# Slots in token order, three early gathers and six late tiles in a fused attention and two-MLP kernel

## The chip, the core and the metric

One core of a Trainium2 chip runs the whole program. The metric is the time of one execution in device microseconds (us). A kernel's time is the median of its timed runs; beside them stands one profiled execution, from which all durations of parts are read. The engines are TensorE (PE; PEld is its weight load), VectorE (DVE), ScalarE (ACT), GpSimd (POOL) and SyncE (SP, here an issuer of DMAs).

## The reference, cut to what matters

Three parts follow each other. Attention between x (8 batches of 512 tokens) and a state of 32 rows per batch gives 8 x 544 = 4352 rows of 512 numbers: 512 x rows and then 32 state rows for each batch. A softplus MLP (512 to 2048 to 512) runs over all of them. Then each row is given to one of eight experts and goes through that expert's MLP:

```python
logits = x @ w_gate
order = np.argsort(-logits.flatten())
for idx in order:
    tok, e = (int(idx) // E, int(idx) % E)
    if assigned[tok] >= 0 or counts[e] >= cap:
        continue
    assigned[tok] = e
    counts[e] += 1
...
for e in range(E):
    mask = assigned == e
    h = np.maximum(x[mask] @ w1[e], 0.0)
    out[mask] = h @ w2[e]
```

With cap = 544, each expert gets exactly 544 rows. The order of the rows inside one expert is free: they are gathered, worked on, and written back to their places.

## The kernel before

**Main loop.** The first MLP runs over 128 slots s = 16 b + ft (8 batches, 16 tiles of 128 hidden columns each), and over 16 state tiles that hold the 256 state rows of all batches. A slot computes h (mlp1), softplus g in steps on ACT and DVE, splits g in a high and a low part (g_hi on ACT or DVE, g_lo at L557 on POOL or DVE), and adds three matmuls of 512 columns to each of four outputs (mlp2: hi x hi, lo x hi, hi x lo).

**Tail.** The second matmuls of the last LATE = 4 slots (12 each) and of the state tiles are held back: mlp2_rest() issues them one at a time. State tiles come as two passes of 16 (j = 0, 1 for the two halves of the state rows, 3 matmuls a tile, L582, L584, L586). When pass j is finished, y_state(j) copies the result to SBUF (L637, DVE) and writes it to y_d in DRAM in four pieces (L640, SP for j = 0, SP and ACT for j = 1). split(i + 1) computes g_hi and g_lo of the next tile when tile i starts.

**Routing.** route(ph) finds the next expert and its 544 rows by a search over seven digits of a threshold, a chain of short DVE steps (v, mk, df, ...) and small matmuls (L1044 counts, L1061 sums). Then finish() turns the mask of the chosen rows into slots: M2 holds the rows surely chosen and, beside them, the ties at the threshold; matmuls with a triangular matrix give each row its rank; four DVE operations make the slot sl, two shifts split it, and ohl, a17 and R follow. R's 17 matmuls (L928) sum up to ixs and idx, the list of row numbers (one yield, "slots", lies between R and these matmuls). The route of the first expert runs between the held-back matmuls: step i is followed by BETWEEN[i] of them; at "slots" all that are left are issued (rest(99)), before R's matmuls.

**Gathers and experts.** gather(0) issues indirect DMAs on POOL: xg piece a gets the rows of y_d named by column a of idx (five pieces: 4 x 128 and 32). Each piece is turned by four transposes (L1186), ACT makes yTh (L1189) and DVE yTl (L1190). yTh and yTl lie in memory that the finished first MLP used. The expert's weights w1 are loaded by load_w1 (one DMA of 2 MB, L1115) and split in eight pieces, w1h on ACT (L1158) and w1l on POOL or DVE (L1159). An expert then has 16 units of 12 matmuls (L1277), (ft, half); unit u of the first expert needs piece u for u below 7. The second matmul of the expert (L1322) follows.

**What sets the order.** Strings written by hand: BEGIN is worked off before the first unit, AFTER[u] behind unit u. In the kernel before, x is gather of pieces 0 and 1, y the gather of 2 to 4 and the load of w2, s a w1 piece with w1l on POOL, v one with w1l on DVE, t a group of transposes, r the next step of route(1). Each engine executes its instructions in the order in which they stand; a wait holds up all that stands behind it on that engine.

## Time and profile before

| | us |
|---|---|
| Median of 3 runs | 1209.81 |
| Lowest and highest | 1209.26, 1211.1 |
| The profiled execution | 1206.22 |
| Its span (first to last instruction) | 1204.4 |
| TensorE busy | 1148.3 (95%) |
| DVE, ACT, POOL busy | 649.8, 640.6, 484.4 |
| Mean granted clock of TensorE | 0.99 |

The span leaves 1.82 us of the profiled execution outside. All places in time below are us from the span's start. The tail begins at about 701, the first expert's units at 755.8. In rows in order of time, a start and a duration are followed by engine, line, operation, output <- inputs and, where the engine sat idle before, by how long and what released it. Matmul durations overlap: two that follow each other start 0.23 us apart (512 columns at full clock), though each lasts 0.39.

### The profile page before, as it was taken

To read this page: it belongs to the slowest core of one execution; us is meant where nothing else is said; L and a number is where in the kernel's file an instruction comes from. 1 tells how busy PE (TensorE), PEld (TensorE's weight loads), DVE (VectorE), ACT (ScalarE), POOL (GpSimd) and SP (SyncE) were. 2 spreads that over 40 slices of the span, in tenths; PEclk is the share of its full clock that TensorE was granted. 3 is DMA by queue.
4 is the path that set the end of the run, shared out by engine and by line. 5 is a ranking of instruction groups with operands and counts; after the bars stand their busy time and mean duration, and the time that the engine had idled before them with its cause. 6 is when DMAs were issued, how large, how long until landed. Compare 5 with 4: busy or idle time off the path is not lost.

```text
span 1204.4 us, 21169 instructions
## 1 busy us (share of the span) xinstructions
PE 1148.3 (95%) x8256; PEld 905.3 (75%) x8256; DVE 649.8 (54%) x1744; ACT 640.6 (53%) x1277; POOL 484.4 (40%) x472
## 2 busy tenths in 40 slices
PE   4798999999999999999999997999999999999996
PEld 1566677777677777777777765979797988889895
DVE  6998435463363533634434266776685767641120
ACT  3776666666676666766766732533333333343330
POOL 0333423232232232322344435645646555556531
PEclk9998999999999999999999999899999999999999
DMA  7454021111201201012000003250523425234201
GB/s 245 141 193 142 1 71 36 54 53 36 70 1 42 64 29 55 23 36 70 1 18 19 1 18 123 91 197 25 200 82 143 136 80 180 106 119 133 92 18 38
DMA packets 51060, 95.77 MB, mean 80 GB/s; under 512 B 4624, under 2 KB 19088, under 8 KB 50960
## 3 DMA queue, kind: packets, MB, share of 16 engines
q1 hardware_dynamic: 45232, 76.46, 19.4%
q0 software_dynamic: 5632, 17.83, 4.4%
q8 instruction: 65, 1.06, 0.4%
q14 instruction: 35, 0.29, 0.1%
q10 hardware_dynamic: 96, 0.13, 0.0%
HBM read 76.58 MB, written 17.83 MB: 78 GB/s over the span
## 4 chain that ended last, share of the span: by engine, by line
PE 79%; DVE 10%; issue 6%; POOL 2%; ACT 1%; DMA 1%; SPq 0%; POOLq 0%; DVEq 0%; ACTq 0%
PE p_h L491 13%; PE p_y L1322 12%; PE p_y L575 8%; PE p_y L577 8%; PE p_y L579 8%; PE p_y L1277 7%; PE p_h L1277 6%; PE p_bg L460 2%; PE p_y L582 2%; PE p_bg L502 2%; PE p_y L586 2%; PE p_y L584 2%; PE p_h L1186 1%; DVE c_a L198 1%; PE p_bg L1044 1%
## 5 line engine op out<-in xcount | busy, mean ns | idle before, releaser
L557 POOL TENSOR_TENSOR g_lo<-g,g_hi 128x512 fp32r<-128x512 f32 x127 | 164.1, 1293 | 324.6 <-ACT g_hi L554 268.1
L575 PE MATMUL p_y<-g_hi,wo_hi 128*128 128x512 f32 x448 | 185.6, 414 | 0.0
L577 PE MATMUL p_y<-g_hi,wo_lo 128*128 128x512 f32 x448 | 178.3, 398 | 3.6 <-POOL wo_lo L237 3.6
L579 PE MATMUL p_y<-g_lo,wo_hi 128*128 128x512 f32 x448 | 176.4, 394 | 0.0
L554 ACT ACTIVATE g_hi<-g 128x512 fp32r<-128x512 f32 x126 | 79.6, 632 | 118.5 <-DVE g L546 84.7
L546 DVE SCALAR_TENSOR_TENSOR g<-p_h,t_sp 128x512 f32<-128x512 f32 x128 | 87.5, 684 | 98.1 <-ACT t_sp L534 97.6
L575 PEld LDWEIGHTS p_y<-g_hi,wo_hi 128*128 128x128 f32 x448 | 85.1, 190 | 49.1 <-ACT t_sp L526 12.6
L1322 PE MATMUL p_y<-w2h,h2h 128*128 128x512 f32 x256 | 105.0, 410 | 0.0
L491 PE MATMUL p_h<-at_hi,P_hi 128*128 128x512 f32 x256 | 103.6, 405 | 1.4 <-DVE g L546 1.4
L491 PE MATMUL p_h<-at_hi,P_lo 128*128 128x512 f32 x256 | 101.6, 397 | 0.0
L491 PE MATMUL p_h<-at_lo,P_hi 128*128 128x512 f32 x256 | 101.5, 397 | 0.0
L1322 PE MATMUL p_y<-w2l,h2h 128*128 128x512 f32 x256 | 101.4, 396 | 0.0
L1322 PE MATMUL p_y<-w2h,h2l 128*128 128x512 f32 x256 | 101.2, 395 | 0.0
L577 PEld LDWEIGHTS p_y<-g_hi,wo_lo 128*128 128x128 f32 x448 | 85.3, 191 | 20.7 <-POOL wo_lo L237 4.9
L579 PEld LDWEIGHTS p_y<-g_lo,wo_hi 128*128 128x128 f32 x448 | 85.3, 190 | 19.4
L1330 POOL DMA_INDIRECT out_dram<-ot,idx x40 | 38.7, 969 | 143.8 <-ACT ot L1328 72.5
L526 ACT ACTIVATE t_sp<-p_h 128x512 f32<-128x512 f32 x128 | 75.4, 589 | 27.8 <-PE p_h L491 27.0
L1159 POOL TENSOR_TENSOR w2l<-s2w,w2h 128x512 fp32r<-128x512 f32 x64 | 81.6, 1291 | 13.1 <-ACT w2h L1158 12.3
L534 ACT ACTIVATE t_sp<-t_sp 128x512 f32<-128x512 f32 x128 | 80.9, 632 | 4.1
L1159 POOL TENSOR_TENSOR w1l<-s1w,w1h 128x512 fp32r<-128x512 f32 x63 | 80.1, 1297 | 6.0 <-ACT w1h L1158 5.2
L533 ACT ACTIVATE t_sp<-t_sp 128x512 f32<-128x512 f32 x128 | 80.7, 631 | 2.3
L1277 PE MATMUL p_y<-yTl,w1h 128*128 128x288 f32 (+1 forms) x256 | 77.3, 302 | 0.0
(282 smaller groups left out, 2611.0 us busy)
## 6 DMA issues: line engine op xcount, KB each, us to landing
s1w<-in_moe_w_dram SPq DMA_DIRECT2D x8, 2048.0 KB, 8.3
s2w<-in_moe_w_dram SPq DMA_DIRECT2D x8, 2048.0 KB, 9.1
st<-in_moe_w_in_dram SPq DMA_DIRECT2D x16, 512.0 KB, 4.1
xT<-in_x_t_dram SPq DMA_DIRECT2D x16, 512.0 KB, 4.4
st<-in_moe_w_out_dram SPq DMA_DIRECT2D x16, 512.0 KB, 3.8
xt<-in_x_s_dram SPq DMA_DIRECT2D x8, 1024.0 KB, 5.5
y_d<-yz SPq DMA_DIRECT2D x48, 128.0 KB, 3.5
y_d<-s_g SPq DMA_DIRECT2D x8, 128.0 KB, 2.5
```

What stands on the lines that cost most here:

```text
L491: PE.matmul(h, l[:, f0:f0 + 128], r[:, par, :], start=(n == 0), stop=(n == 5))
L533: A.activation(t, t, AF.Exp, scale=-1.0)
L534: A.activation(t, t, AF.Ln, bias=1.0)
L546: V.scalar_tensor_tensor(g[:, :w], hps.pop(s)[:, :w], 0.0, tsp.pop(s)[:, :w], op0=OP.max, op1=OP.add)
L554: A.activation(hi[:, c], g[:, c], AF.Copy)
L557: (G if on[1] == "G" else V).tensor_tensor(lo[:, c], g[:, c], hi[:, c].bitcast(F32), op=OP.subtract)
L575: PE.matmul(yb[j], wo_hi[:, ft, c], hi, start=st, stop=False)
L577: PE.matmul(yb[j], wo_lo[:, ft, c], hi, start=False, stop=False)
L579: PE.matmul(yb[j], wo_hi[:, ft, c], lo, start=False, stop=sp)
L1159: eng.tensor_tensor(lo, src, hi.bitcast(F32), op=OP.subtract)
L1277: PE.matmul(p[:, :w], l[:, k, f], r[:, k, c], start=(n == 0), stop=(n == 11))
L1322: PE.matmul(p, l[:, ft, c], r[:, ft, :], start=(n == 0), stop=(n == 23))
```

## The change

Slots are given out in the order of rows, ties included. M2 gets one more column between the two halves, tri2 replaces the corner of the triangular matrix that ranked all ties behind all sure rows, and finish() computes the slot with a constant SKIP, in six short DVE operations where there were four (room, val, sl2, sl3, sl, U). So the first expert's first three pieces hold rows from the front of y_d.

Three gathers of the first expert are therefore issued earlier: at "slots" ROWS = 20 held-back matmuls are issued instead of all, 30 are left over for behind R's matmuls, gather(0, range(3)) follows idx at once, then four steps of route(1) with four matmuls each (ROUND), then the rest of the matmuls and y_state(1). The rows of y_d that y_state(1) will write (state rows of batches 4 to 7) are filled with zeros once, in the main loop, by four DMAs on SP.

LATE is 6; the two further g tiles lie in the pool of the state tiles, with their own places in LATE_ON. BEGIN becomes "sttrr", AFTER and W2_FROM change; x is now one gather (pieces 3 and 4), w the load of w2.

```diff
-    LATE = 4
+    LATE = 6
...
-        if s < NX:
+        if 0 <= s - (NX - LATE) < 2:
+            g = stash["pool"].tile([128, 512], F32, name="g2", bufs=2)
+        elif s < NX:
             g = wk.tile([128, 512], F32, name="g", bufs=5)
...
-    LATE_ON = ("VG", "AG", "VG", "AV")
+    LATE_ON = ("VG", "AG", "VG", "AG", "AG", "AV")
...
+            for i in range(4, 8):
+                r0 = i * TB + S
+                SP.dma_start(y_d[r0:r0 + NS], first[3].rearrange("p a b -> p (a b)").bitcast(F32)[0:NS, 0:DM])
...
-        V.scalar_tensor_tensor(val, p[:, 0:2 * NJ], float(CAP), M2, op0=OP.is_lt, op1=OP.mult)
-        sl2 = rt.tile([128, 2 * NJ], F32, name="sl2")
-        V.scalar_tensor_tensor(sl2, p[:, 0:2 * NJ], 1.0, val, op0=OP.add, op1=OP.mult)
-        V.tensor_tensor(U, U, val[:, NJ:], op=OP.subtract)
-        V.scalar_tensor_tensor(sl, sl2[:, 0:NJ], -1.0, sl2[:, NJ:], op0=OP.add, op1=OP.add)
+        room = rt.tile([128, 1], F32, name="room")
+        V.tensor_scalar(room, p[:, NJ:NJ + 1], -1.0, float(CAP), op0=OP.mult, op1=OP.add)
+        val = rt.tile([128, NJ], F32, name="val")
+        V.scalar_tensor_tensor(val, p[:, NJ + 1:2 * NJ + 1], room, M2[:, NJ + 1:], op0=OP.is_lt, op1=OP.mult)
+        sl2 = rt.tile([128, NJ], F32, name="sl2")
+        V.scalar_tensor_tensor(sl2, M2[:, 0:NJ], -float(SKIP), p[:, 0:NJ], op0=OP.mult, op1=OP.add)
+        V.scalar_tensor_tensor(sl3, p[:, NJ + 1:2 * NJ + 1], room, sl2, op0=OP.min, op1=OP.add)
+        V.scalar_tensor_tensor(sl, val, -float(SKIP), sl3, op0=OP.mult, op1=OP.add)
+        V.tensor_tensor(U, U, val, op=OP.subtract)
...
+    ROWS, ROUND = 20, (4, 4, 4, 4)
...
-        rest(99 if at_ == "slots" else BETWEEN[i])
+        rest(ROWS if at_ == "slots" else BETWEEN[i])
         if 0 in RES and 0 not in W1S:
             load_w1(0)
+
+    gather(0, range(3))
+    rgen = routing()
+    for n in ROUND:
+        next(rgen)
+        rest(n)
...
-    BEGIN = "xrrrrrrsyrrttrst"
-    AFTER = ("ssvsrr", "r", "r", "s", "t", "", "t", "s")
-    W2_FROM = 5
+    BEGIN = "sttrr"
+    AFTER = ("rvxsrrw", "rxrs", "rtr", "s", "ts", "rs", "t", "s")
+    W2_FROM = 7
```

Lines after the edits are shifted: L557 becomes L567, L640 L650, L928 L944, L1044 L1064, L1061 L1081, L1133 L1153, L1159 L1186, L1186 L1213, L1190 L1217, L1277 L1303, and L582 to L586 become L592 to L596.

POOL, from the last tiles of the held-back work on: xg<-y_d are the gathers. Before:

```order
L557 TENSOR_TENSOR g_lo<-g,g_hi 128x512
L557 TENSOR_TENSOR g_lo<-s_g,g_hi 128x128 x32
L1133 DMA xg<-y_d,idx 128x512 x2
L1159 TENSOR_TENSOR w1l<-s1w,w1h 128x4x128
L1133 DMA xg<-y_d,idx 128x512 x2
L1133 DMA xg<-y_d,idx 32x512
L1122 MEMSET s2w 1x1
L1159 TENSOR_TENSOR w1l<-s1w,w1h 128x4x128 x5
```

After:

```order
L567 TENSOR_TENSOR g_lo<-g,g_hi 128x512 x3
L567 TENSOR_TENSOR g_lo<-s_g,g_hi 128x128 x27
L1153 DMA xg<-y_d,idx 128x512 x3
L567 TENSOR_TENSOR g_lo<-s_g,g_hi 128x128 x5
L1186 TENSOR_TENSOR w1l<-s1w,w1h 128x4x128
L1153 DMA xg<-y_d,idx 128x512
L1186 TENSOR_TENSOR w1l<-s1w,w1h 128x4x128
L1142 MEMSET s2w 1x1
L1153 DMA xg<-y_d,idx 32x512
L1186 TENSOR_TENSOR w1l<-s1w,w1h 128x4x128 x5
```

The first three gathers now stand ahead of the g_lo of the last five state tiles, and the other two singly between the weight pieces.

TensorE, at the start of the first expert: L1186 and L1213 are transposes of gathered rows, L1061 and L1081 the sum that ends a digit of route(1), L1277 and L1303 the units. Before:

```order
L1186 MATMUL p_h<-ident,xg 128x128 x8
L1061 LDWEIGHTS taken_79
L1061 MATMUL p_bg_7529<-sat_6909,taken_79 128x8
L1186 MATMUL p_h<-ident,xg 128x128 x4
L1277 MATMUL p_y_7553<-yTh,w1h 128x256
L1277 MATMUL p_y_7553<-yTl,w1h 128x256
L1277 MATMUL p_y_7553<-yTh,w1l 128x256
```

After (p_y_7526 is the first unit, p_h the second):

```order
L1303 MATMUL p_y_7526<-yTl,w1h 128x256
L1303 MATMUL p_y_7526<-yTh,w1l 128x256
L1081 LDWEIGHTS taken_79
L1081 MATMUL p_bg_7554<-sat_6886,taken_79 128x8
L1303 MATMUL p_h<-yTh,w1h 128x256
L1303 MATMUL p_h<-yTl,w1h 128x256
L1303 MATMUL p_h<-yTh,w1l 128x256
```

The sum of route(1)'s first digit has moved from ahead of the last transposes to behind the first unit.

DVE, at the first weight piece that it splits itself (w1l), with the answer of that digit (df to mk) ahead of it. Before:

```order
L1190 TENSOR_TENSOR yTl<-p_h,yTh 128x4x128 x2
L1063 TENSOR_REDUCE df<-p_bg_7529 128x1
L1019 TENSOR_SCALAR p_bg_6890<-df 128x1
L74 TENSOR_SCALAR tmp<-p_bg_6890 128x1
L75 SCALAR_TENSOR_TENSOR p_bg_6890<-tmp,p_bg_6890 128x1
L1023 TENSOR_TENSOR p_bg_6890<-pat,p_bg_6890 128x31
L1031 TENSOR_TENSOR mk_6905<-v,p_bg_6890 128x34x31
L1190 TENSOR_TENSOR yTl<-p_h,yTh 128x4x128
L1159 TENSOR_TENSOR w1l<-s1w,w1h 128x4x128
```

After:

```order
L647 COPY yt<-p_y_7337 128x512
L1217 TENSOR_TENSOR yTl<-p_h,yTh 128x4x128 x2
L1069 SCALAR_TENSOR_TENSOR pe<-p_bg_7527,rem_6874 31x8
L1071 SCALAR_TENSOR_TENSOR pe<-p_bg_7527,pe 31x8 x2
L1072 TENSOR_TENSOR sat_6886<-p_bg_7527,pe 31x8
L1083 TENSOR_REDUCE df<-p_bg_7554 128x1
L1039 TENSOR_SCALAR p_bg_6867<-df 128x1
L75 TENSOR_SCALAR tmp<-p_bg_6867 128x1
L76 SCALAR_TENSOR_TENSOR p_bg_6867<-tmp,p_bg_6867 128x1
L1043 TENSOR_TENSOR p_bg_6867<-pat,p_bg_6867 128x31
L1051 TENSOR_TENSOR mk_6882<-v,p_bg_6867 128x34x31
L1186 TENSOR_TENSOR w1l<-s1w,w1h 128x4x128
L1309 SCALAR_TENSOR_TENSOR h2l<-p_y_7526,h2h 128x256
```

Piece 1's w1l stands directly behind the digit's mk; before, DVE's first w1l came behind the third yTl and was piece 5.

## Rows read from the trace of the kernel before

**Rows 1.** Busy us of each engine (x instructions), TensorE's clock, DMA share and GB/s, by stretch.

```profile
640.00:701.00 61.00, 59.34 (x368) 45.88 (x367) 21.01 (x44) 42.31 (x89) 21.82 (x17) 1.00 0.01 2
701.00:743.60 42.60, 40.80 (x238) 28.85 (x239) 31.88 (x126) 11.48 (x35) 21.47 (x45) 1.00 0.21 75
743.60:755.80 12.20, 3.98 (x39) 3.12 (x39) 7.75 (x24) 2.34 (x4) 7.14 (x8) 0.73 0.42 127
755.80:790.00 34.20, 34.15 (x337) 31.93 (x336) 25.19 (x100) 15.63 (x37) 17.78 (x16) 0.95 0.20 66
```

**Rows 2.** TensorE in order of time: start, us, line, out<-in, [idle before <- releaser].

```profile
742.94 0.40 PE L584 MATMUL p_y<-wo_lo,g_hi 128*128 128x512 f32 x1
743.17 0.39 PE L586 MATMUL p_y<-wo_hi,g_lo 128*128 128x512 f32 x1
743.49 0.73 PE L928 MATMUL p_bg<-R,ohl 128*64 128x68 bf16 x17
749.18 0.41 PE L1044 MATMUL p_bg<-ohu,mk 128*128 128x32 bf16 x9 [4.95 <-DVE mk L1031]
751.28 1.12 PE L1186 MATMUL p_h<-ident,xg 128*128 128x128 f32 x4 [1.70 <-DMA xg<-y_d,idx]
...
755.10 1.08 PE L1186 MATMUL p_h<-ident,xg 128*128 128x128 f32 x4 [1.28 <-DMA xg<-y_d,idx]
755.83 0.56 PE L1277 MATMUL p_y<-yTh,w1h 128*128 128x256 f32 x1
...
758.54 0.47 PE L1044 MATMUL p_bg<-ohu,mk 128*128 128x32 bf16 x9
...
760.66 0.18 PE L1061 MATMUL p_bg<-sat,taken 128*128 128x8 bf16 x1
```

**Rows 3.** DVE in order of time, same columns.

```profile
741.51 1.42 DVE L959 TENSOR_TENSOR R<-a,p_bg 128x578 bf16<-128x578 f32 x2
743.60 0.69 DVE L637 COPY yt<-p_y 128x512 f32<-128x512 f32 x1 [0.67 <-PE p_y L586]
...
755.09 0.15 DVE L1063 TENSOR_REDUCE df<-p_bg 128x1 f32<-128x8 f32 x1
...
756.10 1.26 DVE L1031 TENSOR_TENSOR mk<-v,p_bg 128x1054 bf16<-128x1054 f32 x1
...
758.40 0.84 DVE L1159 TENSOR_TENSOR w1l<-s1w,w1h 128x512 fp32r<-128x512 f32 x1 [0.46 <-ACT w1h L1158]
```

**Rows 4.** POOL in order of time, same columns.

```profile
742.43 0.46 POOL L557 TENSOR_TENSOR g_lo<-s_g,g_hi 128x128 fp32r<-128x128 f32 x1 [0.23 <-ACT g_hi L554]
747.56 1.40 POOL L1133 DMA_INDIRECT xg<-y_d,idx  x1 [4.67 <-DVE cu L1004]
749.27 0.95 POOL L1133 DMA_INDIRECT xg<-y_d,idx  x1 [0.31 <-issue]
...
757.41 4.24 POOL L1159 TENSOR_TENSOR w1l<-s1w,w1h 128x512 fp32r<-128x512 f32 x3 [0.99 <-ACT w1h L1158]
```

**Rows 5.** The state rows' writes (L640): SP in order of time; the line's landing.

```profile
731.53 1.74 SPq L640 DMA_DIRECT2D y_d<-yt  x4
...
DMA to landing us min/median/max: 1.6/1.7/2.0
```

**Rows 6.** The second expert's idx on DVE, and its first gather on POOL.

```profile
798.17 0.67 DVE L971 SCALAR_TENSOR_TENSOR idx<-ixs 32x5 int32<-32x5 f32 x4
...
799.63 1.01 POOL L1133 DMA_INDIRECT xg<-y_d,idx  x1 [3.26 <-issue]
```

**Rows 7.** Two stretches at half clock, columns as in Rows 1.

```profile
97.40:100.75 3.35, 3.35 (x12) 2.68 (x9) 3.26 (x7) 2.05 (x4) 1.29 (x1) 0.50 0.48 159
...
749.50:759.50 10.00, 6.73 (x41) 5.91 (x38) 5.66 (x16) 4.66 (x9) 8.22 (x9) 0.50 0.68 199
```

**Rows 8.** ACT in order of time, columns as in Rows 2.

```profile
753.85 0.60 ACT L1189 ACTIVATE yTh<-p_h 128x512 fp32r<-128x512 f32 x1 [0.77 <-PE p_bg L1061]
754.34 0.62 ACT L1158 ACTIVATE w1h<-s1w 128x512 fp32r<-128x512 f32 x1
```

39 lines of the change are left out of this document (22 added, 17 removed).

## The prediction

> **What bounds the kernel now.** I read the stretches around the change first [rows 1], then the orders of time of each engine inside the worst stretch. TensorE is the bound nearly everywhere: it is busy for 59.34 of the 61 us before the tail and for 34.15 of 34.20 us once the first expert runs. The exception is the 12.2 us from 743.6 to 755.8, where it is busy for 3.98 at a mean granted clock of 0.73. That hole is the object of the change. In order of time [rows 2]: the last state matmul is issued at 742.94 + 0.23 = 743.17, R's 17 small matmuls follow, then TensorE is idle for 4.95 us until DVE has route(1)'s first mask mk, 1.70 us until the first gather has landed, and 1.28 us until the third has. The first unit starts at 755.83, and the second ends at 760.66 (its L1061). On the other side [rows 3], DVE has R at 741.51 + 1.42 = 742.93, copies y_state(1) at 743.60, and the first of five gathers is issued by POOL at 747.56, with 1.40 us for the first and 0.95 plus a gap of 0.31 for another [rows 4]. After 755.8 no weight piece holds TensorE up.
>
> The question is which waits the early gathers take away, and what they now stand in front of.
>
> **The main loop's end.** Two more x tiles are held back: 2 x 4 x 3 = 24 matmuls at 0.23 (two neighbours of [rows 2]), 5.5 us that leave the slots before 701 and run after them. These slots keep all their work on ACT and DVE, so part of the 5.5 becomes idle. Bounds: nothing, or as much again as the whole stretch has now (61.00 - 59.34 = 1.66 in [rows 1]). I take 1.1, since the last slots already wait. The first late matmul then comes 4.4 us sooner than the 701.0 at which the tail now begins [rows 1], at about 696.6.
>
> **Routing of the first expert.** Its steps hang on late and state matmuls by the unchanged BETWEEN, so it moves forward by the same 4.4; finish() has six small operations ahead of the shifts where it had four, 0.4 more at most. R is ready at 742.93 - 4.4 + 0.4 = 738.9. TensorE has 144 + 24 - 30 = 138 matmuls ahead of R instead of 144, so it is there 1.4 us too soon and waits about 1.3. R's matmuls take 0.73 [rows 2]: 739.7.
>
> **The gathers on POOL.** Gather 0 needs idx and the landing of y_state(0), whose copy now stands on DVE right behind R: 0.69 [rows 3], so 739.6. Its four writes take SP 1.74 to issue [rows 5], the last from 741.0, and land 1.7 later (median; 1.6 to 2.0), 742.7. From idx to a gather there are 0.79 us in the later expert (798.17 + 0.67 to 799.63 [rows 6]); so gather 0 starts at 743.5. By idx alone it would be 741.8: R's matmuls, two short operations and 0.67 for idx, plus 0.79. Three gathers take 1.01 to 1.40 for the first [rows 4, 6], 0.95 and 0.31 for the others, 3.5 to 3.9; I take 3.7: 747.2. **The g_lo of the last five state tiles now stand behind them**, in POOL's queue. One takes 0.46 [rows 4], so the sixth tile is ready at 747.7. TensorE has had 15 matmuls that were ready, until 739.7 + 15 x 0.23 = 743.2. It waits 4.5 us here, about what it waited for mk before. The last 15 matmuls then end their issue (E') at 750.9 at full clock. The idle stretch of 4.95 us [rows 2] is followed by 10 us at a granted clock of 0.50, the lower level of 1.2 GHz, and another place of the trace shows 3.35 us at 0.50 between full-speed stretches [rows 7]. 3.35 us at half clock costs these 15 matmuls 1.6: E' = 752.5. The new wait is nearest to the one of 4.95, so I take that.
>
> The first gather had 1.40 us while DVE's mk ran beside it, another 0.95 [rows 4]; POOL's spans are rough, and one instance doesn't show why. The Trainium skill (SBUF — State Buffer, SBUF: two separate sides) says that gathers issued from GpSimd can't have their descriptors written while certain VectorE operations hold a port that both share. By that rule each of the three gathers beside route(1)'s DVE operations could take 1.40, so 1.1 us more for the three, and the sum below would be 7.1 instead of 6.0; the trace agrees with it once and not for the others.
>
> **From the last state matmul to the first unit.** The first unit needs the memory of the finished MLP, and so the landing of y_state(1), in ACT's and DVE's queues: copy from E' + 0.43 (743.17 to 743.60), 0.69, two issues of 0.43 on each of two queues (a quarter of 1.74), 1.7 to 2.0 to land: E' + 3.4. Then two yTh of 0.60 [rows 8] and, for the second matmul, DVE's yTl behind the second of them, which I take as long as a yTh: the unit starts at about E' + 5.2, with the two groups of transposes and route(1)'s count inside that time. That is 757.7, or 756.1 at full clock, against 755.83. The wait on mk and the two on gathers are gone; in their place stand the wait behind POOL and this landing. So the gathers' time is hidden, but the chain that was beside it is not. The unit takes 2.7 at half clock, as before (755.83 to 758.54 [rows 2]), or half of that, 1.4, at full: I take half clock, 760.4.
>
> **The second unit.** Its third matmul needs piece 1's w1l, on DVE, and that stands behind the whole answer of route(1)'s digit, which needs the L1081 that TensorE issues after the first unit. From the first unit's end: df and four small ones 1.0 (755.09 to 756.10), mk 1.26, w1l 0.84 [rows 3], 3.1 with the matmuls hidden. Before, the same chain ran under the last transposes. Two of its twelve matmuls don't wait, so it ends 3.1 + 1.3 later, at 764.8, 4.1 after 760.66; at full clock throughout 762.0, 1.3 after.
>
> **Behind it.** The group of transposes of chunk 2, done before 755.83 so far, is still to do: 0.5 (0.73 by 755.10 to 755.83 at half clock [rows 2], half of that at full). Weight pieces 4 and 5 are split one unit ahead only, each w1h behind the yTh of chunks 2 and 3 on ACT, so a unit needs 0.60 + 0.62 [rows 8] + 1.41 (a third of 4.24 [rows 4]) behind the transposes: 2.6 for unit 5, and for unit 4 that less a unit of 1.4. Bounds: nothing, as before, or 3.8. I take 1.4, because ACT and POOL can catch up while TensorE waits ahead of these units, but their orders let them use only part of that time.
>
> **Sum.** 4.1 + 0.5 + 1.4 = 6.0 over the profiled execution, 1206.22 + 6.0 = 1212.2 there (its span is 1204.4, with 1.82 outside, unchanged). The median of the runs lies 3.59 above that execution, at 1209.81, so I forecast 1215.8. Its bounds: 1.3 + 0.5 + 0 = 1.8, at full clock and without piece waits, to 4.1 + 0.7 + 3.8 = 8.6: 1211.6 to 1218.4. The load of w2 is issued behind the first unit instead of ahead of it, on SP, and its first piece is split two units later (W2_FROM 7 for 5); the second matmul needs it only behind sixteen units, so I cost it at nothing, and if that cover were too short, at most the delay of two units, 2.9. The zero writes, the wider M2 by one column and the SKIP arithmetic I cost at nothing: the writes go out in the main loop, where SP and the DMA engines have slack; without that cover a write's landing, 1.7.
>
> **Rivals.** (A, forecast) TensorE waits behind the gathers and at piece 1: 1215.8, chance 0.45.
>
> (B, faster) The routing chain is bound by TensorE's queue, not by its own latency, between 701 and 743. For it: DVE is busy for only 31.88 of these 42.6 us [rows 1], so its steps wait for matmuls. Against: BETWEEN is unchanged, so the same number of matmuls stands ahead of each step. Each us by which R is ready sooner starts the gathers a us sooner; at 4.5 sooner, with gather 0 at 739.0, the wait behind POOL is gone, the clock stays up (1.6 for the state tiles and 1.3 for the first unit), and the pieces are in time. 6.0 - 4.5 - 1.6 - 1.3 - 1.4 = -2.8: 1207.0. It is faster from about there, and not with less. Chance 0.24. The Trainium skill (DMA: Bandwidth & Descriptors, Rules for kernel authors) advises just this: issue a DMA early, compute, and wait for it late. By that rule the 1.70 and 1.28 us waited for gathers [rows 2] would be a gain of 3.0; the rows bear it out for the landing alone, not for POOL's queue.
>
> (C, no difference) The hole only changes its owner: full clock and no piece waits, the lower bound of 1.8: 1211.6, and up to 1.7 less if the gathers go with idx (741.8 for 743.5). Chance 0.18.
>
> (D, much slower) The pieces hold TensorE at every unit, with unit 3 waiting for h2l too, and half clock comes back after each wait: 8.6 and up to 3 more, 1219 to 1221; or gather 0 starts no sooner than 747, that is, the change doesn't do what it says, and all the rest shifts by 3. Chance 0.13.
>
> **How the numbers follow.** 0.2%, 2.4 us, is about what a measurement of this kernel can tell from no change. Faster is B, 0.24; C is within, 0.18; slower is A and D, 0.58. The range from 1205.5 to 1219.5 holds A, C, nearly all of B and a part of D. A's own range is 1211.6 to 1218.4.
>
> **What would show it.** In the changed profile: TensorE idle for about 4.5 us, released by POOL's g_lo, some 15 state matmuls behind R's; gathers from about 743.5, ahead of five g_lo; the last state matmul near 751 to 752.5; the first unit 5 us after it; an idle of about 3 us inside the second unit, released by DVE's w1l; a granted clock of 0.50 around 748 to 752. Wrong would be: gathers from 740 on, state matmuls without a gap, or units that follow each other without waits.

## The result and the profile after

The kernel after takes 1228.89 us (median of 5, 1227.38 to 1230.49) beside 1210.85 for the kernel before (median of 5): a ratio of 1.0150, 95% interval 1.0136 to 1.0165. It is slower by 18.0 us; the forecast was slower by 6.0, at 1215.8, and the time lies above the range that ended at 1219.5. The profiled execution of the kernel after took 1230.49, with a span of 1228.7; it is the slowest of its five.

First the place where the hole of [rows 1] was. The stretches of the kernel after, columns as in [rows 1] (busy us of TensorE, weight load, DVE, ACT and POOL, then the granted clock, the DMA share and GB/s):

```profile
739.00:744.00 5.00, 4.61 (x34) 3.67 (x34) 4.46 (x15) 1.56 (x5) 1.67 (x5) 1.00 0.48 164
744.00:748.00 4.00, 0.25 (x2) 0.00 (x0) 1.16 (x1) 0.00 (x0) 3.37 (x4) 0.78 0.43 107
748.00:753.30 5.30, 5.15 (x13) 4.08 (x14) 0.00 (x0) 0.94 (x3) 1.88 (x5) 0.52 0.20 68
753.30:760.00 6.70, 2.72 (x27) 2.32 (x26) 2.62 (x7) 2.75 (x5) 2.89 (x3) 0.99 0.24 61
760.00:772.90 12.90, 9.73 (x52) 9.06 (x51) 6.50 (x20) 2.53 (x6) 2.80 (x4) 0.50 0.53 178
772.90:780.00 7.10, 5.02 (x42) 4.32 (x42) 4.37 (x14) 2.44 (x6) 3.58 (x3) 0.96 0.00 1
780.00:784.00 4.00, 4.00 (x30) 3.57 (x28) 1.15 (x6) 0.39 (x1) 0.22 (x1) 0.57 0.00 0
784.00:800.43 16.43, 16.06 (x141) 15.26 (x140) 11.09 (x50) 8.31 (x19) 11.57 (x10) 1.00 0.01 2
```

Where [rows 1] had one hole of 12.2 us and then 34 us without a gap, there is now TensorE idle in 744 to 748, in 753.3 to 760, and again and again until 780; and the granted clock is 0.50, the lower level, for 12.9 us in a row behind 760, and 0.57 once more at 780. Before, it was back at full speed at 759.5 [rows 7].

TensorE's waits, in order of time (start, us, line, out<-in, idle time before and its releaser):

```profile
739.39 0.73 PE L944 MATMUL p_bg<-R,ohl 128*64 128x68 bf16 x17 [1.28 <-DVE R L980]
748.15 0.80 PE L596 MATMUL p_y<-wo_hi,g_lo 128*128 128x512 f32 x1 [3.90 <-POOL g_lo L567]
758.27 0.38 PE L1303 MATMUL p_y<-yTh,w1h 128*128 128x256 f32 x1 [3.52 <-ACT yTh L1216]
759.11 0.39 PE L1303 MATMUL p_y<-yTl,w1h 128*128 128x256 f32 x1 [0.45 <-DVE yTl L1217]
764.20 0.58 PE L1303 MATMUL p_h<-yTh,w1l 128*128 128x256 f32 x1 [2.33 <-DVE w1l L1186]
767.81 0.19 PE L1081 MATMUL p_bg<-sat,taken 128*128 128x8 bf16 x1 [0.84 <-DVE sat L1072]
777.68 0.38 PE L1303 MATMUL p_h<-yTh,w1h 128*128 128x256 f32 x1 [1.21 <-ACT w1h L1185]
779.03 0.39 PE L1303 MATMUL p_h<-yTh,w1l 128*128 128x256 f32 x1 [0.85 <-POOL w1l L1186]
784.37 0.40 PE L1303 MATMUL p_h<-yTh,w1h 128*128 128x288 f32 x1 [0.37 <-ACT yTh L1216]
```

The 4.95 us on mk, and the 1.70 and 1.28 on gathers [rows 2], are gone. In their place stand a wait behind POOL's queue (3.90), one on the last yTh (3.52), and six waits inside the first units.

All engines in order of time, the rows at the two places that the prediction named, POOL's queue and piece 1 on DVE:

```profile
743.95 1.14 POOL L1153 DMA_INDIRECT xg<-y_d,idx  x1 [0.81 <-DVE cu L1024]
745.40 0.96 POOL L1153 DMA_INDIRECT xg<-y_d,idx  x1 [0.31 <-issue]
746.66 0.95 POOL L1153 DMA_INDIRECT xg<-y_d,idx  x1 [0.31 <-issue]
747.63 0.88 POOL L567 TENSOR_TENSOR g_lo<-s_g,g_hi 128x128 fp32r<-128x128 f32 x2
...
762.29 1.25 DVE L1051 TENSOR_TENSOR mk<-v,p_bg 128x1054 bf16<-128x1054 f32 x1
763.46 0.68 DVE L1186 TENSOR_TENSOR w1l<-s1w,w1h 128x512 fp32r<-128x512 f32 x1
```

The gathers go ahead of the g_lo on POOL, and the sixth state tile's third matmul starts at 748.15 when its g_lo is there; piece 1's w1l comes on DVE right behind the digit's mk, and the second unit's third matmul at 764.20. ACT's yTh, which the first unit waits for, itself waits for the landing of y_state(1):

```profile
757.13 1.09 ACT L1216 ACTIVATE yTh<-p_h 128x512 fp32r<-128x512 f32 x2 [1.14 <-DMA y_d<-yt]
```

**Ledger.** The first unit starts at 758.27 instead of 755.83 (+2.4). From there to the next expert's first unit it takes 73.14 us instead of 59.62 (+13.5): +12.3 in the sixteen units, which end at 800.43 instead of 785.72, and +1.2 behind them. (That 1.2 goes with the one step of route(1) that the new strings do more: e9 below does one step less, and it is gone there.) The third expert takes 63.62 instead of 57.01 (+6.6), the fourth 58.26 instead of 56.61 (+1.7); all others differ by 0.5 at most. The sum, 24.3, is the difference of the two spans. By the medians the loss is 18.0, since the profiled execution of the kernel before, 1206.22, lies 4.6 below its median of 1210.85, and that of the kernel after 1.6 above its own; this is taken up with the last two experiments.

### The profile page after: what moved, and what is told of

The parts are those of the page before. It is cut to its first block, busy times and chain, and to the rows that moved or that the text cites. A ratio compares the mean times of both kernels' runs of the same rounds, so it can differ in the third digit from the quotient of the medians.

```text
span 1228.7 us, 21199 instructions
## 1 busy us (share of the span) xinstructions
PE 1158.4 (94%) x8256; PEld 911.3 (74%) x8256; DVE 652.7 (53%) x1763; ACT 640.2 (52%) x1277; POOL 485.5 (40%) x473
## 4 chain that ended last, share of the span: by engine, by line
PE 77%; DVE 11%; issue 6%; POOL 2%; ACT 2%; DMA 1%; another core or an unknown queue 0%; SPq 0%; POOLq 0%; ACTq 0%; DVEq 0%
PE p_h L499 12%; PE p_y L1348 12%; PE p_y L585 8%; PE p_y L587 8%; PE p_y L589 7%; PE p_y L1303 7%; PE p_h L1303 6%; PE p_bg L468 2%; PE p_y L592 2%; PE p_y L596 2%; PE p_bg L510 2%; PE p_y L594 1%; PE p_h L1213 1%; DVE c_a L206 1%; PE p_bg L1064 1%
## 5 line engine op out<-in xcount | busy, mean ns | idle before, releaser
L567 POOL TENSOR_TENSOR g_lo<-g,g_hi 128x512 fp32r<-128x512 f32 x127 | 164.9, 1299 | 323.9 <-ACT g_hi L564 267.5
L1186 POOL TENSOR_TENSOR w1l<-s1w,w1h 128x512 fp32r<-128x512 f32 x63 | 79.8, 1289 | 28.4 <-ACT w1h L1185 27.7
L1186 POOL TENSOR_TENSOR w2l<-s2w,w2h 128x512 fp32r<-128x512 f32 x64 | 81.9, 1296 | 12.0 <-ACT w2h L1185 11.2
L1303 PE MATMUL p_y<-yTh,w1h 128*128 128x288 f32 (+1 forms) x256 | 78.2, 305 | 3.9 <-ACT yTh L1216 3.9
```

The source lines that it names most:

```text
L567: (G if on[1] == "G" else V).tensor_tensor(lo[:, c], g[:, c], hi[:, c].bitcast(F32), op=OP.subtract)
L1186: eng.tensor_tensor(lo, src, hi.bitcast(F32), op=OP.subtract)
L1303: PE.matmul(p[:, :w], l[:, k, f], r[:, k, c], start=(n == 0), stop=(n == 11))
```

## The experiments

The runs came in five groups, and those of one group ran on one chip beside the same runs of the kernel before; the first two groups had the same chip. Ratios are to these, with 95% intervals; a difference of two ratios is uncertain by some 0.002, or 2.5 us. "First unit" and "first expert" are the start of the first unit and the time from there to the next expert's first unit, from the profile of each run (kernel before: 755.83 and 59.62; after: 758.27 and 73.14). A profile is a single execution. Three more runs below, e6, e13 and e18, have the order of the kernel after in the tail and the first units; their first units start at 757.00, 756.40 and 757.12, and their first experts take 71.62, 73.73 and 73.73. So two profiles of one order can differ by some 2 us at either place, and gains of that size are read from the ratios.

### What the four parts of the change cost

**e4_no_early** keeps slots in token order, the zero writes and six late tiles, and takes the early gathers and the new strings back.

```diff
-    ROWS, ROUND = 20, (4, 4, 4, 4)
+    ROWS, ROUND = 99, (4, 4, 4, 4)
...
-    gather(0, range(3))
     rgen = routing()
-    for n in ROUND:
-        next(rgen)
-        rest(n)
...
-    BEGIN = "sttrr"
-    AFTER = ("rvxsrrw", "rxrs", "rtr", "s", "ts", "rs", "t", "s")
-    W2_FROM = 7
+    BEGIN = "xrrrrrrsyrrttrst"
+    AFTER = ("ssvsrr", "r", "r", "s", "t", "", "t", "s")
+    W2_FROM = 5
...
-                gather(0, [more.pop(0)])
+                gather(0, range(2))
             else:
+                gather(0, range(2, 5))
                 load_w2(0)
```

> The changed kernel without its early gathers: all held-back matmuls at the old place, gathers and strings as before the change. What is left of the change is the slots in token order, the zero writes and six late tiles for four. All theories: within 2.4 us of the kernel before, 1209 to 1213, with the tail starting 4.4 us sooner and the hole as long as before. If the slot arithmetic, the zero writes or the idle that the two tiles leave behind cost something themselves, it is slower than 1213.

Measured: 1209.23 beside 1209.07, ratio 1.0003 (0.9993 to 1.0012); first unit 756.99, first expert 59.10. TensorE waits as before, first on mk:

```profile
750.24 0.42 PE L1064 MATMUL p_bg<-ohu,mk 128*128 128x32 bf16 x9 [4.95 <-DVE mk L1051]
```

So the slots, the zero writes and the longer tail cost nothing that can be measured, as the prediction had it, but the longer tail brings nothing either. The whole loss belongs to the early gathers (with the four steps of route(1) that go along with them) and the strings.

**e3_old_strings** keeps the early gathers too, and takes only the strings back.

```diff
-    BEGIN = "sttrr"
-    AFTER = ("rvxsrrw", "rxrs", "rtr", "s", "ts", "rs", "t", "s")
-    W2_FROM = 7
+    BEGIN = "rrsyrrttrst"
+    AFTER = ("ssvsrr", "r", "r", "s", "t", "", "t", "s")
+    W2_FROM = 5
...
             else:
+                gather(0, range(3, 5))
                 load_w2(0)
```

> The changed kernel with BEGIN, AFTER and W2_FROM as before the change (but for the three gathers and the four steps of route(1) that are already done): five weight pieces, three groups of transposes and the digit's answer stand ahead of the first or second unit again. Early gathers stay ahead of the state's last tiles. Theory Q: the units run without waits once begun, and most of the 13.5 us that the first expert takes longer (73.1 for 59.6) comes back: 1216 to 1220. Theory P: the wait behind the gathers stays and only the 5 us of idle inside the units go: 1223 to 1225.

Measured: 1215.06, ratio 1.0050 (1.0033 to 1.0067); first unit 757.67, first expert 61.75. From ratios: the strings cost 0.0100, some 12 us, and the early gathers by themselves 0.0047, some 5.7. In the profiles the first unit starts within 0.6 us of where it does with the new strings, but the first expert is 11.4 us shorter. What the new strings did is thus behind the first unit, not ahead of it.

### The early gathers: POOL's queue, and the landing

**e1_lo_on_dve** takes the g_lo of the last five state tiles from POOL to DVE, so that the gathers stand in front of none of them.

```diff
-                        LATE_ON[i] if i < LATE else "AG")
+                        LATE_ON[i] if i < LATE else "AV" if i >= len(todo) - 5 else "AG")
```

> The changed kernel, with the low parts (g_lo) of the last five state tiles on VectorE instead of on GpSimd, so that no gather stands ahead of them. Theory P (GpSimd's queue is the main cause): TensorE's wait of 3.90 us behind R goes to under 1 us, the ten state matmuls that ran at half clock run at full, the first unit starts 4 to 6 us sooner (by 754), and the kernel is 4 to 6 us faster than the changed one, at about 1223 to 1225. Theory Q (the new strings for the first units are the main cause): the wait goes, but the first units still stand behind the digit's answer and single pieces, at half clock until about 773, and the kernel gains 2 us or less, 1227.

Measured: 1225.85, ratio 1.0134 (1.0117 to 1.0151); first unit 754.64, first expert 73.75. The wait behind POOL is gone, and the next one is longer:

```profile
745.84 0.50 PE L596 MATMUL p_y<-wo_hi,g_lo 128*128 128x512 f32 x1 [0.72 <-DVE g_lo L567]
754.64 0.58 PE L1303 MATMUL p_y<-yTh,w1h 128*128 128x256 f32 x1 [4.41 <-ACT yTh L1216]
```

```profile
739.00:750.00 11.00, 9.20 (x61) 7.15 (x62) 7.73 (x21) 2.49 (x8) 5.16 (x7) 1.00 0.45 146
750.00:756.00 6.00, 1.34 (x13) 0.94 (x10) 1.77 (x5) 2.75 (x5) 2.51 (x3) 0.79 0.24 61
756.00:772.00 16.00, 12.80 (x77) 11.92 (x76) 8.17 (x28) 3.06 (x7) 4.43 (x5) 0.55 0.46 148
```

The queue is what the 3.90 us were, and without it the clock stays up until 750. From R's matmuls to the first unit it takes 15.1 us, where the kernel after, e6, e13 and e18 take 18.1 to 19.0. But these 3 to 4 us became only some 2 us in the ratio (0.0016, which is within its uncertainty): the units behind still run at 0.55, with the same waits.

**e5_old_strings_lo_dve** is e3 with the edit of e1.

> The changed kernel with the strings of before (as the third experiment) and the last five state tiles' g_lo on VectorE (as the first). With the strings of before the early gathers cost 5.8 us over the kernel without them (1215.06 against 1209.23). If that is the wait behind GpSimd's queue, 3.90 us and the half clock after it, this kernel is 3 to 5 us faster than the third, 1210 to 1212. If it is what stands behind, transposes, yTh and yTl between the state's landing and the first unit, the gain is under 1.5 us and the waits only move: 1214.

Measured: 1212.38, ratio 1.0017 (1.0007 to 1.0026); first unit 755.74, first expert 61.73. From 1.0050 to 1.0017: with the old strings the queue's wait was worth about two thirds of what the early gathers cost, 0.0033 of 0.0047, each uncertain by 0.002. (Their profiles don't show it: that of e3 is the fastest of its four executions, 1211.85 for 1214.40 to 1215.84.)

**e10_own_rows** lets y_state(1)'s copy lie in rows of xg that are not yet used, so that the first yTh, which takes the memory of the finished MLP, doesn't wait for the landing of its writes.

```diff
-        V.tensor_copy(t[:, 0].rearrange("p (q j c) -> p q j c", q=4, j=4), ordered(yb[j]))
+        t = into[0][:, 4] if j else t[:, 0]
+        V.tensor_copy(t.rearrange("p (q j c) -> p q j c", q=4, j=4), ordered(yb[j]))
...
```

> The changed kernel with y_state(1)'s copy in the place of gathered piece 4, which is fetched later anyway, instead of in the finished MLP's memory. yTh, yTl and the first unit then don't wait for the landing of the state's rows, only gathers 3 and 4 do. By the chain of the prediction (copy, issue, landing 3.4 of the 5.2 us behind the last state matmul) the first unit starts 2.5 to 3 us sooner, at 755.5, and the kernel is 2 to 3 us faster, 1226 to 1227. If the digit's answer and the pieces set the pace of the first units anyway, the gain is under 1 us.

Measured: 1227.34, ratio 1.0139 (1.0122 to 1.0156); first unit 757.12, first expert 72.10. The wait on yTh falls from 3.52 to 2.27:

```profile
757.12 0.58 PE L1304 MATMUL p_y<-yTh,w1h 128*128 128x256 f32 x1 [2.27 <-ACT yTh L1217]
```

The other profiles of that order have 3.46 to 3.52. So the landing that the prediction put in the chain was there and held the unit up by 1.2 us; the rest of that wait is the chain of transposes, yTh and w1h on ACT. In the time it can't be told: 0.0011 of the ratio is within the uncertainty.

**e11_old_strings_lo_own** is e5 with the edit of e10.

> The fifth experiment (strings of before, the last five g_lo on VectorE) with y_state(1)'s copy in the place of gathered piece 4 as well. What is left of the early gathers' cost there is a wait of 4.66 us for yTl, and so for the landing, ahead of the third group of transposes. If that is the last thing in front of the units, the wait goes under 2.5 us and the kernel comes to 1209 to 1210 where the fifth had 1212.4: no slower than the kernel before, or 1 us faster. If DVE's digit steps take its place, 1211 to 1212.

Measured: 1212.08, ratio 1.0013 (1.0004 to 1.0023); first unit 754.48, first expert 64.32. That is neither 1209 to 1210 nor told from e5. The wait for yTl only fell from 4.66 to 3.63. The first unit starts 1.3 us sooner than in e5 and the expert takes 2.6 more. The wait inside the units is no longer than in e5 (2.38 and 2.61 us, both for DVE's sat), but the first 12.5 us of the units run at a granted clock of 0.65, where those of e5 run at 0.92: what is won ahead of the units is lost to the clock inside them.

### The first units: pieces, and the clock

**e2_piece_first** splits piece 1 ahead of the digit's answer instead of behind it: one pair of letters.

```diff
-    AFTER = ("rvxsrrw", "rxrs", "rtr", "s", "ts", "rs", "t", "s")
+    AFTER = ("vrxsrrw", "rxrs", "rtr", "s", "ts", "rs", "t", "s")
```

> The changed kernel, with only the first two letters of AFTER[0] swapped (vr for rv): VectorE splits weight piece 1 before it answers route(1)'s digit, not behind. Theory Q: the second unit's wait of 2.33 us for w1l goes, the units behind start 2 to 3 us sooner, and the kernel is 2 to 4 us faster, 1225 to 1227. Theory P: the digit's answer is only late elsewhere, the next count waits for it instead, and the gain is under 1 us.

Measured: 1224.30, ratio 1.0124 (1.0107 to 1.0141); first unit 758.25, first expert 67.07 instead of 73.14. The clock:

```profile
758.00:760.00 2.00, 1.29 (x8) 1.10 (x9) 1.86 (x7) 1.24 (x3) 1.25 (x2) 0.97 0.30 68
760.00:765.00 5.00, 4.16 (x30) 3.92 (x30) 4.32 (x13) 1.28 (x3) 3.03 (x4) 0.67 0.63 202
765.00:780.00 15.00, 11.97 (x102) 10.49 (x103) 9.16 (x29) 5.66 (x13) 4.69 (x4) 1.00 0.26 88
```

The wait of 2.33 on w1l is gone, and in the profile the first expert is 6.1 us shorter, not 2.3: without this wait the clock is back at 1.00 from 765 on, where the kernel after has 0.50 until 772.9. By the ratios the gain is smaller, 0.0026 or some 3 us; the mean granted clock of the profiled execution, 0.987, is the highest of e2's four (the others have 0.984 and 0.985), so this profile shows less half clock than the others had. The waits of later pieces are still there (1.20, 0.85, 0.37, and 0.34 and 0.27 new).

**e7_warm** leaves the order on the other engines as it is and fills three of TensorE's waits with matmuls whose results are not read: 14 of 512 columns ahead of the state tiles that wait behind POOL (three held-back matmuls go ahead of these), 56 of 128 columns ahead of the first unit, and 36 behind it.

```diff
-    for n in ROUND:
+    for i, n in enumerate(ROUND):
         next(rgen)
         rest(n)
+        if i == 0:
+            rest(3)
+            p = bank("y2")
+            for _ in range(14):
+                PE.matmul(p, wo_hi[:, 0, 0:128], wo_hi[:, 0], start=True, stop=True)
...
+    def warm(n):
+        p = bank("y2")
+        for _ in range(n):
+            PE.matmul(p[:, 0:128], ones_b, tri, start=True, stop=True)
+    warm(56)
...
                 begin(AFTER[u] if u < 8 else "")
+                if u == 0:
+                    warm(36)
```

> The changed kernel with matmuls on constants, whose results nobody reads, where TensorE waits: 14 of 512 columns ahead of the wait for the sixth state tile's g_lo, 56 of 128 columns ahead of the first unit, 36 ahead of the second. They are shorter than the waits, so that they delay nothing. If the granted clock of 0.50 after the waits costs what the matmul spacings say (0.43 for 0.23 on ten state matmuls, 0.21 for 0.12 on four units), the stretch from 748 to 774 runs at full clock and the kernel is 4 to 6 us faster, 1223 to 1225. If the waits of the other engines set the pace there anyway, the gain is under 2 us.

Measured: 1225.43, ratio 1.0124 (1.0107 to 1.0141); first unit 757.02, first expert 68.44. The clock of the same stretches:

```profile
739.00:757.00 18.00, 15.48 (x134) 13.03 (x134) 6.56 (x17) 4.24 (x12) 8.62 (x13) 1.00 0.34 104
757.00:772.00 15.00, 12.39 (x125) 11.02 (x125) 10.59 (x35) 4.09 (x10) 5.21 (x6) 1.00 0.53 163
772.00:797.00 25.00, 22.65 (x244) 20.98 (x244) 15.72 (x69) 10.96 (x25) 14.06 (x12) 1.00 0.01 2
```

With the clock at 1.00 throughout, the first unit is 1.3 us sooner and the first expert 4.7 us shorter than in the profile of the kernel after, 6.0 in all. Beside the profile of e6, which ran in the same group, it is 3.2 in all. By the ratios it is 0.0026, some 3 us, beside the kernel after, and 0.0037, some 4.5 us, beside e6. So the half clock cost some 3 to 6 us; the one profile puts it at the upper end.

**e8_pieces_ahead** splits three pieces before the first unit instead of one, and piece 3 on DVE first of all behind it. (Pieces count from 0. So the one that DVE splits in the kernel before is piece 4, the fifth, and not piece 5, as the section on the change has it.)

```diff
-    BEGIN = "sttrr"
-    AFTER = ("rvxsrrw", "rxrs", "rtr", "s", "ts", "rs", "t", "s")
+    BEGIN = "sssttrr"
+    AFTER = ("vxrrrsw", "rxrs", "rtr", "s", "t", "rs", "t", "")
```

> The changed kernel with the weight pieces one to two units earlier: three of them ahead of the first unit on GpSimd, piece 3 on VectorE ahead of the digit's answer, the rest one place earlier; gathers, transposes and routing as changed. Theory Q: the waits of the second unit (2.33) and of the sixth (1.21 and 0.85) go, with the half clock that they keep up, and the kernel is 6 to 9 us faster than the changed one, 1220 to 1223, below the second experiment's 1224.3. If the order of the digit's steps and transposes matters as much, it stays above 1223.

Measured: 1221.57, ratio 1.0089 (1.0073 to 1.0106); first unit 757.74, first expert 64.58. Between the first unit and the end of the sixteenth only 0.25, 0.84, 0.33 and 0.37 us of waiting are left, and the half clock ends before 766:

```profile
757.00:766.00 9.00, 7.17 (x44) 6.51 (x45) 6.50 (x22) 3.00 (x7) 7.07 (x7) 0.66 0.37 106
766.00:791.00 25.00, 24.30 (x222) 23.03 (x221) 18.43 (x73) 11.34 (x26) 12.91 (x11) 1.00 0.17 61
```

Of the 13.5 us that the first expert lost, 8.6 come back in the profile by the order of the pieces alone; the medians of e6 and e8, of one group, differ by 8.4. And they cost nothing ahead of it: the first unit is not later.

### The third expert

In the kernel after, DVE stands still for 4.95 us in the third expert although the counts it waits for (L1064) had ended on TensorE 4.5 us before; ACT's ot and SP's load of s2w start 3 us after the tail's last matmul (it ended at 916.85). The releaser of two of these is one that the profile can't name ("remote"). The kernel after, rows of all engines in order of time (SPq is SP's DMA issue):

```profile
916.16 0.98 POOL L1153 DMA_INDIRECT xg<-y_d,idx  x1 [14.37 <-DVE idx L992]
919.83 1.11 ACT L1337 ACTIVATE ot<-p_y 32x128 f32<-32x128 f32 x4 [4.44 <-remote]
919.88 0.37 SPq L1143 DMA_DIRECT2D s2w<-in_moe_w_dram  x1
920.03 0.39 PE L1064 MATMUL p_bg<-ohu,mk 128*128 128x32 bf16 x9 [0.69 <-DVE mk L1051]
924.93 0.17 DVE L1069 SCALAR_TENSOR_TENSOR pe<-p_bg,rem 31x8 f32<-31x8 f32 x1 [4.95 <-remote]
925.73 0.19 PE L1081 MATMUL p_bg<-sat,taken 128*128 128x8 bf16 x1 [4.28 <-DVE sat L1072]
```

**e6_code_shift** puts 64 more DVE instructions into slots 32 to 95, against the guess that the place of the instructions in the program decides.

```diff
+    shift = const.tile([1, 1], F32, name="shift")
...
+        if s >= 32 and s < 96:
+            V.memset(shift, 0.0)
```

> The changed kernel with 64 one-element memsets more on VectorE, one in each slot from 32 to 95, which nothing waits for. The third expert takes 63.6 us instead of 57.0 in the changed kernel and in the first two experiments, with VectorE idle for 4.95 us ahead of an L1069 whose only input, a count of TensorE, had been there since 920.4. Theory C (a delivery of code, or something else that hangs on the place in VectorE's program): with all instructions 64 places later the 4.95 us go or turn up at another place, the third expert takes 57 to 59 us, and the kernel is 3 to 6.5 us faster than the changed one if they go. Theory D (the data traffic at that time: weights and gathers together): the place in the program doesn't matter, and nothing changes, 1228 to 1229.

Measured: 1229.96, ratio 1.0161 (1.0144 to 1.0178); third expert 62.72, with a wait on DVE of 4.95 us again. The shift changes nothing that these numbers can tell.

**e9_one_step_less** takes one step of route(1) out of AFTER, so that all later steps of the routes come one place later, as with the strings of before.

```diff
-    AFTER = ("rvxsrrw", "rxrs", "rtr", "s", "ts", "rs", "t", "s")
+    AFTER = ("rvxsrrw", "rxrs", "rtr", "s", "ts", "s", "t", "s")
```

> The changed kernel with one step of route(1) less behind the sixth unit (AFTER[5] s for rs), so that 13 steps are done by the eighth unit, as before the change, instead of 14; every later step comes one place later. Theory E (the wait of 4.95 us in the third expert hangs on where the steps of the routes fall against the units): it goes, the third expert takes 57 to 58 us as in the kernel before and in the third experiment, and the kernel is 5 to 6.5 us faster than the changed one, 1222.5 to 1224. Theory F (it hangs on the early gathers or the new strings otherwise): it stays, at 1228 to 1229.

Measured: 1224.35, ratio 1.0112 (1.0095 to 1.0129); third expert 57.04, fourth 60.06, with a wait of 2.26 us of the same kind there. Theory E was right on the third expert; part of what it won there came back in the fourth. On this chip the place of the route's steps is worth some 4.5 us by the ratios (0.0038), or 3.0 beside e10, which ran in the same group.

**e12_ahead_lo_own** puts together e8, e1, e10 and e9.

> All mendings of the changed kernel at once: pieces ahead as in the eighth experiment, the last five g_lo on VectorE, y_state(1)'s copy in the place of piece 4, one step of route(1) less. If the causes add up (1221.6 - 3 - 2.5 - 5.5), about 1210.5, within 2 us of the kernel before; if they overlap in the same waits, 1212 to 1216.

Measured: 1211.16, ratio 1.0011 (1.0001 to 1.0020); first unit 754.46, first expert 63.45, fourth 58.77. The four edits bring back nearly everything, and still nothing is won against the kernel before: the first unit is 1.4 us sooner, the first expert 3.8 longer.

**e13_hold** tries the next guess, that the next expert's gathers do it by falling on the tail's matmuls: from the eleventh unit on until the tail rows' scatter is issued, they are held back.

```diff
-            if len(RES.get(q, ())) == 2 and q not in XG and q not in YT:
+            if len(RES.get(q, ())) == 2 and q not in XG and q not in YT and not held[0]:
...
+            held[0] = u >= 10
...
             scat.append(st)
+            held[0] = False
```

> The kernel after, with one change: from the eleventh unit of an expert until the scatter of its tail rows has been issued on POOL, the five gathers for the next expert are not issued (they then stand behind that scatter). Theory (the next gathers on POOL and their transfers, when they fall on the tail matmuls of the expert, make TensorE's signals arrive 3 to 4.9 us late): in the third expert the gathers move from 916 to after the tail, DVE's wait of 4.95 us and PE's of 4.28 us go, the third expert takes 57 to 58.5 us instead of 63.62, and the time is 1222.5 to 1225.5. Rival (the place of the count matmuls in the expert is the cause, whatever POOL does): the wait stays above 3 us and the time is 1227 to 1231.

Measured: 1223.57 beside 1205.91, ratio 1.0154 (1.0139 to 1.0170); third expert 57.62, and DVE's wait there is gone. By that profile and the time the theory looked right; but the ratio is that of the kernel after, because the kernel before took 4 us less on this chip than on the earlier ones. The kernel after itself didn't run on this chip.

**e14_ahead_hold**, **e15_ahead_hold_warm** and **e16_old_hold** ran beside it: e12 with held gathers; the same with 72 matmuls of 128 columns, results not read, ahead of the first unit; e11 with held gathers.

> The kernel of the pieces ahead, with the state's remainders on DVE, its own rows and one route step less, plus the held gathers. Theory: its fourth and fifth experts, 58.77 and 57.75 us (56.61 and 56.96 before the change), come to 56.6 to 57.3 each, so 1.5 to 3 us go from 1211.2: 1208 to 1210. Rival (the gathers have no part): 1210.5 to 1212.

> The same, with 72 matmuls of 128 columns whose results are not read ahead of the first unit of the first expert, in its wait of 4.4 us. Theory (the half clock of 753 to 761 is due to that wait): clock 1.00 there, the first units 2 us shorter, 1206 to 1208.5. Rival (the wait itself, not the clock, is all there is to gain, and the extra matmuls delay the first unit): 1208 to 1211, no better than without them.

> The kernel with the strings of before, early gathers, remainders on DVE and own rows, plus the held gathers. Its fourth and fifth experts took 60.39 and 57.73 us (56.61 and 56.96 before the change). Theory (the gathers on the tail's matmuls): they come to 56.6 to 57.3 each, so some 3 to 4 us go from 1212.1: 1208 to 1209.5. Rival (the gathers have no part): 1211.5 to 1213.

Measured: e14 1208.98, ratio 1.0026 (1.0017 to 1.0035); e15 1209.49, 1.0029 (1.0018 to 1.0040); e16 1209.65, 1.0031 (1.0020 to 1.0041). No wait of the unnamed kind is in their profiles, and the fourth experts take 57.2 to 57.6. The time of e14 lies where the theory put it, that of e16 0.15 above, but beside this chip's 1205.91 they are worse than e12 and e11 were beside theirs. e15 missed its theory. Its stretches around the first unit, and below them those of e14, show why (columns as above):

```profile
749.00:759.80 10.80, 8.77 (x119) 8.11 (x119) 5.47 (x16) 4.96 (x10) 6.96 (x7) 1.00 0.26 74
759.80:764.00 4.20, 3.49 (x18) 3.50 (x18) 2.75 (x10) 0.00 (x0) 1.50 (x2) 0.59 0.92 276
```

```profile
749.00:759.30 10.30, 5.60 (x34) 5.10 (x33) 4.22 (x13) 4.57 (x9) 6.96 (x7) 0.67 0.23 68
759.30:764.00 4.70, 3.54 (x34) 3.02 (x34) 3.78 (x13) 1.04 (x3) 1.48 (x2) 0.99 0.80 271
```

The filled wait keeps the clock up until 759.8, and with two waits of 0.86 and 0.84 us it falls to 0.59, where e14 is back at 0.99. The half clock came later and was shorter, 3.4 us of the units' time for 5.4 in e14, but the units wait 0.7 us more (2.28 in all for 1.55), and the first expert takes 63.24 for 63.31.

**e17_before_hold** is the kernel before with held gathers, **e18_after_again** the kernel after, unchanged, both on a further chip.

> The kernel before, with the next expert's gathers held until the scatter of the tail rows has been issued. In the trace of the kernel before, the gathers fall on the tail matmuls in one expert only, the fourth (952.36 to 958.36). Theory (such a meeting costs, in most executions, though not in the one profiled): 2 to 5 us less than before on the same chip where before takes about 1210, and no difference where it takes about 1206. Rival (the meeting matters only for the order of the kernel after): no difference from before on either.

> The kernel after once more, beside the same runs of the kernel before. Where before takes about 1206, as it did beside the kernel with held gathers (ratio 1.0154): the theory (the gathers on the tail matmuls cost the kernel after 6 us) gives 1228.5 and a ratio of 1.0185 to 1.021; the rival (holding them changed the profiled execution but not the typical one) gives 1.0150, about 1224. Where before takes about 1210, the ratio is 1.015 again and only the other run tells.

Measured: e17 1207.07 beside 1206.27, ratio 1.0006 (0.9997 to 1.0015), no difference, as either theory had it for such a chip, so that it decides nothing; e18 1223.03, ratio 1.0137 (1.0122 to 1.0153). The theory wanted at least 1.0185 for e18 and falls. The same instructions as above, in e18:

```profile
915.59 0.98 POOL L1153 DMA_INDIRECT xg<-y_d,idx  x1 [14.36 <-DVE idx L992]
916.40 1.12 ACT L1337 ACTIVATE ot<-p_y 32x128 f32<-32x128 f32 x4 [1.58 <-PE p_y L1334]
916.45 0.37 SPq L1143 DMA_DIRECT2D s2w<-in_moe_w_dram  x1
919.46 0.39 PE L1064 MATMUL p_bg<-ohu,mk 128*128 128x32 bf16 x9 [0.69 <-DVE mk L1051]
919.89 0.17 DVE L1069 SCALAR_TENSOR_TENSOR pe<-p_bg,rem 31x8 f32<-31x8 f32 x1 [0.48 <-PE p_bg L1064]
```

The gathers lie on the tail's matmuls just as before (first gather 915.59, the tail's last matmul ends at 916.28), and nobody waits. So the meeting alone isn't the cause. What the runs support is a smaller statement. On the chips of the first three groups, where the kernel before takes 1209 to 1211, orders with the longer string show a wait of 4.8 to 5.0 us in the third expert, and those with one step less or the old strings one of 2.1 to 2.3 in the fourth; on the chips of the last two, where the kernel before takes about 1206, neither is there. But all runs on the fourth group's chip and e17 hold the gathers back; e18 alone has neither the hold nor the wait, so that the chip decides, or the time at which a group ran, rests on one trace. The kernel before probably has its share of the wait in its typical executions on the first chips, since it gains about 4 us on the others; its one trace, of 1206.22, doesn't show it, so that is argued and not shown. That trace isn't of one of the timed executions, and the record doesn't say on which chip it was taken; it may simply come from a chip like the last two. What delays TensorE's signals there stays open.

For the change it matters little. On the last chip, without this wait, the kernel after loses 16.8 us by the medians and 17.2 by the spans: 1.3 up to the first unit, 14.1 in the first expert, 2.0 in the sixth, the others together next to nothing.

## Why the prediction was wrong, point by point

**Right: the tail and the route.** The first late matmul was put at 696.6 and came at 696.79, 4.2 us sooner than in the kernel before (701.01), where the prediction had 4.4. The idle of 1.1 us that it took off for this isn't there in one piece: the two idle times right ahead of that matmul, 0.84 and 0.29 us, stand in the trace of the kernel before as well (at 700.08 and 701.01). New are two of 0.21 and 0.16, at 684 and 688; the rest of what is missing from 5.5 is in no idle time that the trace lists. So the size was right, its place wasn't. TensorE was to wait 1.3 us for R and waited 1.28, its matmuls at 739.39 instead of about 739.

**Right: POOL's queue.** The first gather came at 743.95 (743.5), the three took 3.66 us (3.7), the sixth tile's matmul 748.15 (747.7), after a wait of 3.90 (4.5). The wait is shorter because 17 matmuls were ready ahead of it and not 15: the first two of the sixth tile don't need its g_lo. The last state matmul started at 753.27, so that its issue ended at 753.5 (752.5), with the clock at 0.52 meanwhile, as taken from [rows 7]. e1 and e5 show that the queue was the cause. The gather that ran beside DVE's mk took 1.14, the two after it, with DVE idle, 0.96 and 0.95. In the third expert, though, one beside mk took 0.95 as well. The Trainium skill (SBUF — State Buffer, SBUF: two separate sides) says that GpSimd can't write a gather's descriptors while certain VectorE operations hold a port that both share; these rows agree with it by 0.2 us in one place and not in the other. The price of 1.40 each, which the prediction took for that rule from [rows 4] and left out of its sum, was not paid.

**Right: the first unit, its length in part by luck.** It came at 758.27 against 757.7, with the landing of y_state(1) in the chain (e10). It took 2.74 us where the prediction took 2.7 for half clock; but its first matmuls ran at full clock, 0.12 us apart, until 759.8, and the rest of the time is a wait of 0.45 on yTl that had no term.

**Right in cause, short in price: the second unit.** Its third matmul was to wait about 3 us for w1l behind the whole digit on DVE. It did wait, for 2.33 us. But the unit was to end at 764.8 and ended at 766.5: 0.6 us because the first unit came later, and 1.0 because its ten last matmuls came 0.21 us apart, at half clock. The prediction let the half clock end with the first unit.

**The failed step: half clock behind the first unit.** The terms of the sum behind the second unit, 0.5 for transposes and 1.4 for pieces, 1.9 together, take every matmul of the units there at full clock. From the end of the second unit to the end of the sixteenth it took 33.9 us (766.50 to 800.43) where the kernel before took 25.06 (760.66 to 785.72), all of it at full clock:

```profile
760.66:785.72 25.06, 25.01 (x230) 23.89 (x228) 18.39 (x74) 11.23 (x26) 13.71 (x12) 1.00 0.09 34
```

That is 8.9 more, 7 more than forecast. Of these 8.9, waits make 3.3: 1.21 and 0.85 are the term of the pieces, 2.1 for 1.4 and inside its bounds, while 0.84 on the next digit of route(1) and 0.37 on the last yTh had no term. The transposes make some 0.5. The remaining 5 are nearly all matmuls at half clock, 9.6 us of them in 766.5 to 773.5 and in 780.3 to 783.8, which would be 4.8 at full clock. This price has no term in the sum at all, nor, but for the one group of transposes, in its bounds. Rival D named it ("half clock comes back after each wait") and priced it at up to 3, with a chance of 0.13 for the whole rival. e7 measured it by itself, with the part ahead of the first unit: 6.0 us in the profiles, some 3 to 4.5 by the medians. And the wait on w1l is the one that kept the clock down in this profile: with that wait gone the clock was up again by 765 (e2), and with it and two others filled it never fell (e7).

**Not foreseen: what lies behind the first expert.** The prediction let everything after the first expert's units go unchanged. The 1.2 us behind the units of the first expert had no term either; they go with the one step of route(1) more (e9). In the profile of the kernel after the third expert lost 6.6 us, on the last chip (e18) 0, with the sixth losing 2.0 there. Part of this may belong to the chip and not to the change, which isn't shown. Where it is absent, in e18, the loss of 17.2 is 15.4 up to the end of the first expert, against 6.0 forecast, so that the failed step is the main one there too.

**The offset.** The forecast added 3.59, the distance of the profiled execution of the kernel before from its median, and took it as constant. What it is isn't shown: it may be the unnamed wait of the third expert's experiments, or the profile may come from a chip on which this kernel takes 1206. It did the forecast no harm, as the ratio of the kernel after differs by 0.0013 only, 1.0150 and 1.0137.

**The rivals.** B (faster) needed gather 0 at 739.0; it came at 743.95, since the landing of the first state rows and the idx came as forecast. So its condition didn't hold; and e1, which takes the wait behind POOL away by other means, is still at 1.0134. The Trainium skill (DMA: Bandwidth & Descriptors, Rules for kernel authors) advises to issue a DMA early and to wait for it late; the waits of 1.70 and 1.28 us for gathers are indeed gone. But e3 against e4 shows the whole move, with the strings of before, as a loss of 5.7 us, most of it in POOL's queue (e5). C (same) would have needed full clock and no piece waits. D (much slower) had the half clock that came back, but not the size: it ended at 1221, and its pieces were to hold every unit, where two units waited for one and none for h2l.
